# Delta-rule attention with two expert layers: filler kept up by a modelled share, group 2 prepared sooner, GpSimd steps told shorter to the planner, y keyed by group parity

## The chip, the cores and the metric

The kernel runs on one core of a Trainium2 chip. The time is device microseconds of one launch. Three runs of the kernel before took 1090.52, 1092.03 and 1093.01 us; the median is 1092.03 us.

## The reference

Three computations stand one behind the other. The first is a recurrence over 768 steps for 4 batches of 8 heads with a head dimension of 48:

```python
k_n = k / (norm(k, axis=-1, keepdims=True) + 1e-06)
for t in range(S):
    y[:, :, t] = einsum('bhd,bhde->bhe', q[:, :, t], state)
    v_old = einsum('bhde,bhd->bhe', state, k_n[:, :, t])
    state = state + beta[:, :, t] * outer(k_n[:, :, t], v[:, :, t] - v_old)
x = y.transpose(0, 2, 1, 3).reshape(3072, 384)
x = (silu(x @ w_gate) * (x @ w_val)) @ w_out        # d_ff 1536
out = elu(x @ w_in) @ w_out2                        # d_ff 2048
```

## The kernel before, in words

**Groups.** The 3072 tokens are taken in 12 groups of 256: 128 steps of two batches, in four parts of 32 steps; even and odd groups have different batches. For each group the attention turns the recurrence into triangular matrices of 32 by 32, one for each head, batch and part, which have to be inverted; then come the products with q, k and v, the state's update, and the transposed output, which is the input of the first expert layer. In the last eight groups the first expert layer takes two groups together. The second expert layer runs at the end, over tiles of 512 tokens.

**The steps of attention**, with the lines that the prediction speaks of. `norms` computes the lengths of the keys on VectorE: the sums at line 589, small Newton steps at 641 to 643, the scaling at 597. `prepare` transposes q and k on TensorE (line 698), forms the products of keys (line 748), masks them on VectorE (line 768), and has GpSimd scale and mask v and the matrices (lines 687, 805, 677, 812). `invert` transposes each matrix in four pieces on VectorE (line 852), then solves on GpSimd: 31 multiplications (line 869) and 31 additions (line 876), each waiting for the one before; this is the "chain" of a group. VectorE then transposes the result back (line 900). Group 0 is an exception: its inverse is made on VectorE in halves, which TensorE joins (lines 917 and 933, the "joining products"). `attention` multiplies with the inverse on TensorE (line 994, "xstep", 64 or 128 products of 32 rows), makes the output's and the state's factors ("gstep", line 1031, with VectorE's additions of q at line 1013), carries the state through the four parts of a group (line 1081, VectorE's update at line 1090), forms y (line 1121, "yall"), which ScalarE copies (line 1129), and transposes it (line 1164), after which it is split into a high and a low part (VectorE's at line 1179).

**Weights.** Weights of the first layer come as 18 tiles of 768 KB, loaded in halves on SP's queue (`load_w`, `half`), four halves in flight at most. Each tile is decoded to two fp32r tensors, a high and a low part: two passes on ScalarE, one on VectorE (line 1274), a copy on ScalarE (line 1284), a subtraction on VectorE (line 1288). From the first tile on, 12 "f-steps" of the expert layer follow for each group (`moe1`): products of the gate and the value half with the input's parts (line 1350, the first product with weights), SiLU on ScalarE (line 1358), the product of both halves on VectorE ("times", line 1361), a split of the result into high and low (ScalarE line 1369, VectorE line 1374), and nine output products (line 1382, "output product" of that step).

**The order.** Nothing of this runs in the order in which the code lists it. Each piece is a step with a priority (`add`), and `Order.run` puts the steps in order on each engine by a model: a step's cost on its engine, when its inputs and buffers come free, and the lowest priority number among those that can start. VectorE, ScalarE, GpSimd, TensorE and SP then each work in the order so found. The cost that is told for a step of the chain is

```python
[("POOL", SLOW[min(g, 3)] * (215 + 1.8 * n), SLOW[min(g, 3)] * (215 + 1.8 * n) + 80, 0, f)]
```

with n elements, `SLOW` being 1.0, 1.5, 1.4 and 1.1 for group 0, 1, 2 and all later ones. The preparation of a group has the priority `att_pri(g) - 5`, that of group 1 has `P1` = 14.7 and thereby stands ahead of the decoding of the weights, which has

```python
decode(n, tag, tk, att_pri(0) + 4.8 + 0.02 * n)
```

The loads of k, q and v of group 2 wait, in the order, for weight tile number `K2` = 5.

**Filler.** Where the model sees TensorE idle before a step, up to a modelled time `UNTIL`, `Order.run` puts products in whose result nobody uses: `fill` (line 1551, a 128x512 product), `quick` (line 1557) and `fill2`. Their number follows from the gap alone. The keys that the planner writes for y, `("yk", a)`, are the same for every group.

## Time and profile before

| | |
|---|---|
| median of three runs | 1092.03 us |
| the profiled execution | 1097.85 us, span 1096.1 us |
| instructions in it | 29901 |
| mean granted TensorE clock | 0.982 |
| DMA over the span | 57.07 MB, mean 52 GB/s |
| TensorE idle, by its own row | 1096.1 - 1077.4 = 18.7 us |

All rows below are of the one profiled execution; its time is 5.8 us over the median. PE is TensorE's matmul, DVE is VectorE, ACT ScalarE, POOL GpSimd, SP the engine that issues loads. "PEclk" is the clock that TensorE was granted as a share of full speed (2.4 GHz). In the timeline a row joins consecutive instructions of one line, and brackets tell the idle time ahead of it and what released it. Line numbers are those of the kernel before; in the changed kernel the same lines stand 23 to 27 lines further down.

### The profile page before, as it was taken

How to read it: one execution, taken by the hardware profiler on the slowest of the kernel's cores; microseconds unless marked ns; L12 is line 12 of the kernel's file. 1: busy time of each engine (PE TensorE's matmuls, PEld its weight loads, DVE VectorE, ACT ScalarE, POOL GpSimd, SP SyncE). 2: the span in 40 equal slices, each digit the busy share in tenths (PEclk: the TensorE clock that was granted, in tenths of full speed). 3: DMA queues.
4: the chain of work that ended last, by engine and by line, in shares of the span. 5: the costliest groups of instructions: out<-in, count | busy, mean ns of one | idle time of the engine just before them, and what ended most of it. 6: DMA issues, size and time to landing. Idle time of an engine off the chain costs nothing.

```text
span 1096.1 us, 29901 instructions
## 1 busy us (share of the span) xinstructions
PE 1077.4 (98%) x12839; PEld 937.1 (85%) x12839; DVE 602.8 (55%) x1178; ACT 537.6 (49%) x1076; POOL 342.2 (31%) x765
## 2 busy tenths in 40 slices
PE   8989999999999999999999999999999999999998
PEld 6678999999988787888777788888888888898887
DVE  7788766666555544556434466546345454444534
ACT  6679554344343433333322577645455454554443
POOL 1685777687770874064540000000000000000000
PEclk9589999999999999999999999999999999999999
DMA  9683131223012201203000456101001010000000
GB/s 164 162 245 103 31 47 31 33 45 58 5 27 35 45 2 38 38 16 60 9 19 2 154 191 198 44 1 48 11 1 58 1 58 1 10 29 1 29 1 29
DMA packets 104949, 57.07 MB, mean 52 GB/s; under 512 B 77392, under 2 KB 97360, under 8 KB 104816
## 3 DMA queue, kind: packets, MB, share of 16 engines
q1 hardware_dynamic: 104816, 55.16, 20.3%
q8 instruction: 100, 1.64, 0.6%
q14 instruction: 33, 0.27, 0.1%
HBM read 45.71 MB, written 9.44 MB: 50 GB/s over the span
## 4 chain that ended last, share of the span: by engine, by line
PE 90%; ACT 3%; DVE 3%; DMA 2%; issue 1%; SPq 0%; DVEq 0%; ACTq 0%
PE gv L1350 26%; PE acc L1382 11%; PE acc L1514 9%; PE gv L1476 9%; PE at L1476 9%; PE at L1514 9%; PE at L1081 3%; PE at L1031 3%; PE at L1382 3%; PE at L698 2%; PE at L994 2%; PE at L1121 1%; PE at L748 1%; DMA w<-in_moe_w_val_dram 1%; PE acc L1551 1%
## 5 line engine op out<-in xcount | busy, mean ns | idle before, releaser
L1350 PE MATMUL gv<-xa,w 128*128 128x512 f32 (+1 forms) x1008 | 218.6, 350 | 2.2 <-DVE hb L1374 1.1
L1350 PEld LDWEIGHTS gv<-xa,w 128*128 128x128 f32 x1008 | 160.3, 190 | 27.6 <-DVE hb L1374 3.2
L1382 PE MATMUL acc<-hb,w 128*128 128x256 f32 (+1 forms) x720 | 155.3, 335 | 0.0
L869 POOL TENSOR_TENSOR ain<-z,ain 128x126 f32<-128x126 f32 (+22 forms) x310 | 120.6, 389 | 67.6 <-DVE ain L852 32.5
L1350 PE MATMUL gv<-xb,w 128*128 128x256 f32 (+1 forms) x720 | 139.4, 327 | 0.0
L876 POOL TENSOR_TENSOR z<-z,ain 128x126 f32<-128x126 f32 (+22 forms) x310 | 128.0, 413 | 23.8
L1361 DVE TENSOR_TENSOR gv<-gv,tb 128x256 f32<-128x256 f32 (+1 forms) x96 | 54.1, 564 | 132.3 <-PE gv L1350 106.7
L1358 ACT ACTIVATE tb<-gv 128x256 f32<-128x256 f32 (+1 forms) x96 | 47.3, 492 | 157.6 <-PE gv L1350 157.4
L1350 PEld LDWEIGHTS gv<-xb,w 128*128 128x128 f32 x720 | 107.8, 190 | 12.6
L1382 PEld LDWEIGHTS acc<-hb,w 128*128 128x128 f32 x720 | 107.2, 191 | 12.7
L1369 ACT CAST hb<-gv 128x256 fp32r<-128x256 f32 (+1 forms) x96 | 46.0, 479 | 108.6 <-DVE gv L1361 105.7
L1374 DVE TENSOR_TENSOR hb<-gv,hb 128x256 fp32r<-128x256 f32 (+1 forms) x96 | 53.3, 555 | 42.4 <-PE at L1382 26.4
L1491 DVE SCALAR_TENSOR_TENSOR hb<-gv,hb 128x512 f32<-128x512 f32 x45 | 31.1, 691 | 81.2 <-ACT hb L1488 81.2
L1482 ACT ACTIVATE hb<-gv 128x512 f32<-128x512 f32 x45 | 26.9, 598 | 79.2 <-PE gv L1476 79.1
L1382 PE MATMUL at<-hb,w 128*128 128x512 f32 x144 | 56.2, 390 | 0.0
L1488 ACT ACTIVATE hb<-hb,zn 128x512 f32<-128x512 f32 x70 | 50.7, 724 | 2.2
L1491 DVE SCALAR_TENSOR_TENSOR hb<-at,hb 128x512 f32<-128x512 f32 x25 | 17.3, 692 | 60.6 <-ACT hb L1488 60.4
L1031 PEld LDWEIGHTS at<-gr,R 32*96 32x96 f32 x1292 | 39.0, 167 | 10.1 <-issue 5.9
L1482 ACT ACTIVATE hb<-at 128x512 f32<-128x512 f32 x25 | 15.0, 600 | 63.0 <-PE at L1476 62.9
L1031 PE MATMUL at<-gr,R 32*96 32x80 f32 x1292 | 44.8, 257 | 0.9 <-ACT lc L1050 0.9
L1485 ACT ACTIVATE hb<-hb 128x512 f32<-128x512 f32 x70 | 44.3, 633 | 2.1
L1476 PE MATMUL at<-lc,w 128*128 128x512 f32 x150 | 42.8, 393 | 0.0
(261 smaller groups left out, 2223.3 us busy)
## 6 DMA issues: line engine op xcount, KB each, us to landing
w<-in_moe_w_out_dram SPq DMA_DIRECT2D x28, 384.0 KB, 4.5
w<-in_moe_w_in_dram SPq DMA_DIRECT2D x16, 384.0 KB, 3.9
w<-in_moe_w_gate_dram SPq DMA_DIRECT2D x12, 384.0 KB, 4.2
w<-in_moe_w_val_dram SPq DMA_DIRECT2D x12, 384.0 KB, 4.7
kq<-in_q_dram SPq DMA_DIRECT2D x11, 384.0 KB, 6.1
x2d<-hb SPq DMA_DIRECT2D x16, 256.0 KB, 2.6
kp<-in_k_dram SPq DMA_DIRECT2D x10, 384.0 KB, 4.4
R<-in_v_dram SPq DMA_DIRECT2D x24, 96.0 KB, 2.2
```

Of the source, the lines that this page charges most:

```text
L869: E.tensor_tensor(out=t, in0=z[:, l:l + 1, x:y].to_broadcast([128, m, y - x]), in1=an[:, l + 1:32, l:l + 1].to_broadcast([128, m, y - x]), ...
L876: E.tensor_tensor(out=z[:, l + 1:32, x:y], in0=z[:, l + 1:32, x:y], in1=t, op=ALU.add)
L1031: PE.matmul(bank[h[c].got[0]][0:96, i:i + 80], lhsT=R[t, u, :], rhs=gr[t, u, o0:o0 + 80], start=True, stop=True, skip_group_check=True)
L1350: PE.matmul(dst, lhsT=wt[:, a_, kk * 128:(kk + 1) * 128], rhs=X[b_][:, :, kk, :] if two else X["one", g][:, b_, kk, :], start=(n == 0), st ...
L1358: A.activation(out=c['s'], in_=gate(0), func=ACTF.Silu)
L1361: V.tensor_tensor(out=gate(1), in0=gate(1), in1=c['s'], op=ALU.mult)
L1374: V.tensor_tensor(out=c['h'][1], in0=gate(1), in1=c['h'][0].bitcast(F32), op=ALU.subtract)
L1382: PE.matmul(sums(d), lhsT=wt[:, a_, d * 128:(d + 1) * 128], rhs=c['h'][b_], start=(f == 0 and n == 0 and (two or d != 1)), stop=(f == F1 - ...
L1476: PE.matmul(x, lhsT=W[f][:, 0, a_, kk * 128:(kk + 1) * 128], rhs=x2[n][b_][:, kk, :], start=(m == 0), stop=(m == 3 * KD - 1))
L1488: A.activation(out=c['r'], in_=c['r'], func=ACTF.Identity, bias=neg1, scale=1.0)
L1491: V.scalar_tensor_tensor(out=c['r'], in0=bank[h.got[0]], scalar=0.0, in1=c['r'], op0=ALU.max, op1=ALU.add)
L1514: PE.matmul(o, lhsT=c['h'][:, b_, t * 128:(t + 1) * 128], rhs=W[f][:, 1][:, a_, :], start=(f == 0 and m == 0), stop=(f == F2 - 1 and m == 2))
```

## The change

The planner keeps a list of what TensorE does in modelled time and weighs each kind of step by a factor (`FULL`). From 20 us of modelled time until the first product of the expert layer, it looks, ahead of each step of the attention, at the last 3413 ns of modelled time; where the weighed share is under `LOWEST` = 0.42 it adds as many fillers as lift it there, whether or not a gap is that long. `SLOW` becomes 1.25 and 1.1 for groups 1 and 2. The preparation of group 2 gets the priority 14.75, ahead of the decoding, and its loads wait for weight tile 6 instead of 5. The keys of y tell odd from even groups. In pairs of groups each product with the gate half is ordered behind the value half's product of the f-step before. `XTWO` is empty and so changes nothing.

```diff
--- before.py
+++ after.py
@@ -69,6 +69,10 @@
     BUSY = 4200.0
     SLOW = 1.8
     COLD = 430.0
+    LOWEST = 0.42
+    SPAN = 3413.0
+    KEEP = 20e3
+    FULL = (1.0, 1.0, 0.5, 0.15, 0.25, 0.2, 0.12, 0.06, 0.05)
 
     def __init__(self):
         self.rng = Random(self.SEED)
@@ -83,6 +87,8 @@
         self.cold = False
         self.last_end = 3e3
         self.since = 0.0
+        self.acts = []
+        self.dense = False
         self.steps = []
         self.last = {}
         self.seen = {}
@@ -165,6 +171,10 @@
     def link(self, b, o):
         b.succ.append(o)
         o.np += 1
+
+    def active(self, t):
+        return sum((min(b, t) - max(a, t - self.SPAN)) * w for a, b, w in self.acts[-60:]
+                   if b > t - self.SPAN and a < t)
 
     def run(self, until):
         self.until = until
@@ -246,6 +256,7 @@
                         self.fetch(t - gap, self.unit * n, 2 * n, True)
                         self.fill(n)
                         self.awake(t - gap, t - gap + self.unit * n)
+                        self.acts.append((t - gap, t - gap + self.unit * n, 1.0))
                         gap -= self.unit * n
                     n = int(self.BLOCK - self.at % self.BLOCK) // 4 * 2 + 4
                     self.fetch(t - gap, 28.0 * n, 2 * n, True)
@@ -254,9 +265,16 @@
                 unit = self.COLD if self.cold else self.unit
                 n = int((self.share if gap < 4000 else self.LONG) * gap / unit +
                         (0.5 if t < self.EARLY and not self.cold else 0.0))
+                keep = not self.dense and t > self.KEEP and o.pri[0] < 1000
+                if keep:
+                    short = self.LOWEST * self.SPAN - self.active(t) - max(0, n) * unit
+                    if short > 0:
+                        n = max(0, n) + int(short / unit + 0.7)
                 if n > 0:
-                    late = self.fetch(t - gap, gap, 2 * n, True)
+                    gap = max(gap, 0.0)
+                    late = self.fetch(t - gap, max(gap, n * unit), 2 * n, True)
                     self.awake(t - gap, t - gap + n * unit)
+                    self.acts.append((t - gap, t - gap + n * unit, 1.0))
                     t = max(t, t - gap + n * unit + late)
                     self.fill(n)
                     kind[0] = k[0]
@@ -281,6 +299,9 @@
                     end = t + lat
                     kind[0] = k[0]
             free[e] = t + occ
+            if e == "PE" and not self.dense:
+                self.acts.append((t, t + occ, self.FULL[k[0]]))
+                self.dense = o.pri[0] >= 1000
             for h in o.need:
                 a = sorted((slot.get(s, 0.0), i) for i, s in enumerate(h.pool)
                            if slot.get(s, 0.0) is not None)[:h.n]
@@ -317,7 +338,7 @@
     KD = DM // 128
     C = 4
     BLOCKED = (0,)
-    SLOW = (1.0, 1.5, 1.4, 1.1)
+    SLOW = (1.0, 1.25, 1.1, 1.1)
     PL1 = 0.5
     ND = 10
     UNTIL = 170e3
@@ -328,13 +349,15 @@
     CALM = 10
     WARM = 8
     P1 = 14.7
+    PREP = {1: P1, 2: 14.75}
     LATE = NW - 2
     LC0 = (NW - 3, NW - 1)
     PAIRS = 4
     THREE = 1
     XSHY = True
+    XTWO = ()
     XDVE = (0,)
-    K2 = 5
+    K2 = 6
     BIG = ()
 
     sb = ctx.enter_context(tc.tile_pool(name="sb", bufs=1))
@@ -979,7 +1002,7 @@
             return f
         o0, q0, k0_ = first_of(g), q_of(g), k_of(g)
         paired = g >= NB - 2 * PAIRS
-        for aa in [(0, 1)] if g and (not paired or XSHY) else [(0,), (1,)]:
+        for aa in [(0, 1)] if g and (not paired or XSHY and g not in XTWO) else [(0,), (1,)]:
             shy = paired and len(aa) == 2
             h = {(a, n): Slots(GB if shy else AT, 1) for a in aa for n in range(2)}
 
@@ -1142,8 +1165,8 @@
                 k0 = state(a, c)[1]
                 rk_ += [k0, (k0, 1)]
             def rest():
-                add(p, act(384, put), r=[h] + (yd if a else []), w=[yk[a], ("yk", a)], use=[h])
-            return 750, f, rk_ + lk[a] + INIT, h, [yk[a], ("yk", a)] + (yd if a else []), rest
+                add(p, act(384, put), r=[h] + (yd if a else []), w=[yk[a], ("yk", g % 2, a)], use=[h])
+            return 750, f, rk_ + lk[a] + INIT, h, [yk[a], ("yk", g % 2, a)] + (yd if a else []), rest
 
         def xtr(a):
             h = Slots(AT, 1)
@@ -1184,7 +1207,7 @@
             def rest():
                 add(p, act(384, hi), r=[h] + kh_, w=[("xh", g % 2, a)] + kh, use=[h])
                 add(p, dvp(384, lo), r=[h, ("xh", g % 2, a)] + kl_, w=[("xl", g % 2, a)] + kl, use=[h])
-            return (370, f, [("yk", a), yk[a]] + (yd if a else []), h,
+            return (370, f, [("yk", g % 2, a), yk[a]] + (yd if a else []), h,
                     kx + ([] if paired else [("xh", g % 2, a), ("xl", g % 2, a)]), rest, 6)
 
         def chains(c):
@@ -1315,6 +1338,7 @@
         if fresh:
             buf['sums'] = Slots(["at3"], 1)
         hs = buf.get('sums')
+        turned = []
 
         def sums(d):
             if two:
@@ -1384,7 +1408,8 @@
                                   skip_group_check=True)
             pp = p + f
             h1 = h[-1]
-            x = add(pp, pe(ns, proj(0), 1), r=xk + wk, w=[(h[0], 0)] + turn(4), need=h[:1] + ([hs] if fresh and f == 0 else []))
+            x = add(pp, pe(ns, proj(0), 1), r=xk + wk, w=[(h[0], 0)] + turn(4), need=h[:1] + ([hs] if fresh and f == 0 else []),
+                    after=turned[-1:])
             mark.setdefault((g, 'm'), x)
             add(P_MOE, act(w, silu), r=[(h[0], 0)], w=[ht] + turn(0), need=[ht], use=h[:1])
             if gs[-1] == NB - 1 and f == F1 - 1:
@@ -1392,6 +1417,8 @@
                     out=sm[2][:, 0:1], in_=neg1, func=ACTF.Exp))], r=["neg1", ht], w=["sm"])
             mark[gs[-1], 'last'] = add(pp, pe(ns, proj(1), 1), r=xk + wk, w=[(h1, 1)] + turn(5), need=h[1:],
                                        use=() if two else h[:1], after=[x])
+            if two:
+                turned.append(mark[gs[-1], 'last'])
             add(P_MOE, dvp(w, times), r=[ht], w=[(h1, 1)] + turn(1), use=[h1, ht])
             after = buf.get(('evac', g - 1), ()) if f == (0 if two else 2) else ()
             add(P_MOE, act(w, hi), r=[(h1, 1)], w=[(hh[0], 0)] + turn(2), need=hh[:1], use=[h1], after=after)
@@ -1586,7 +1613,7 @@
     rows()
     def ahead(g):
         load_k(g, 100 + 10 * g if g > 1 else PL1, [sent[K2]] if g == 2 else [])
-        norms(g, att_pri(g) - 5 if g > 1 else P1)
+        norms(g, PREP.get(g, att_pri(g) - 5))
 
     ahead(1)
     attention(0, att_pri(0) + 1)
@@ -1620,7 +1647,7 @@
         if g:
             if g > 1:
                 load_qv(g, 100 + 10 * g, [sent[K2]] if g == 2 else [])
-            prepare(g, att_pri(g) - 5 if g > 1 else P1)
+            prepare(g, PREP.get(g, att_pri(g) - 5))
             if g + 1 < NB:
                 ahead(g + 1)
             attention(g, att_pri(g) + 1 if g > 1 else P1)
```

What moves on the engines is told by the order of instructions. On VectorE, the place where group 2's inverse is transposed back (line 900; the names with z are the inverse, gv and hb the expert layer's intermediate results), in the kernel before:

```order
L768 TENSOR_TENSOR gr<-at_87,nbs 128x8x2x32
L768 TENSOR_TENSOR gr<-at_88,nbs 128x8x2x32
L1361 TENSOR_TENSOR gv_84<-gv_84,tb_2190 128x256
L1374 TENSOR_TENSOR hb_86_2205<-gv_84,hb_86_2205 128x256
L1361 TENSOR_TENSOR gv_83<-gv_83,tb_2218 128x256
L1374 TENSOR_TENSOR hb_88_2233<-gv_83,hb_88_2233 128x256
L900 STREAM_TRANSPOSE ain<-z_640 128x32x16
L852 STREAM_TRANSPOSE ain<-gr 128x256
```

The same place on VectorE in the changed kernel, where line 900 is now 923, 1274 is 1297, 1288 is 1311, 1361 is 1385 and 1374 is 1398:

```order
L1311 TENSOR_TENSOR w_70_1838<-xb_112,w_70_1838 128x2x384
L1398 TENSOR_TENSOR hb_73_1888<-gv_83,hb_73_1888 128x256
L1297 SCALAR_TENSOR_TENSOR xb_112<-xb_112,w_54_1512 128x768
L1113 TENSOR_TENSOR sv<-at_88,sv 48x2x4x48 x2
L1311 TENSOR_TENSOR w_74_1926<-xb_112,w_74_1926 128x2x384
L1297 SCALAR_TENSOR_TENSOR xb_112<-xb_112,w_57_1530 128x768
L1385 TENSOR_TENSOR gv_84<-gv_84,tb_1954 128x256
L923 STREAM_TRANSPOSE ain<-z_646 128x32x16
L1398 TENSOR_TENSOR hb_77_1984<-gv_84,hb_77_1984 128x256
L1311 TENSOR_TENSOR w_76_1971<-xb_112,w_76_1971 128x2x384
L1385 TENSOR_TENSOR gv_83<-gv_83,tb_1998 128x256
```

Before, the transposition stood behind the results of 14 f-steps, two of them of group 1's layer and all decoding done; now it stands behind 11, ahead of the split of the eleventh result (hb_77) and of the last weight tile's subtraction (w_76).

On TensorE, what stands in front of group 2's xstep (line 994) in the kernel before; acc<-hb is an output product, gv<-xb a first product with weights of group 1's layer:

```order
L1382 MATMUL acc<-hb_82_2081,w_75_1939 128x256 x9
L1350 MATMUL gv_84<-xb_2000,w_14_593 128x256 x18
L1350 MATMUL gv_83<-xb_2000,w_16_601 128x256 x18
L1382 MATMUL acc<-hb_86_2205,w_20_717 128x256 x9
L1350 MATMUL gv_84<-xb_2000,w_25_826 128x256 x18
L994 MATMUL at_86<-gr,ain 32x80 x4
```

In the changed kernel (1350 is 1374, 1382 is 1406, 994 is 1017, 1164 is 1187, 748 is 771), from the last output product of group 0's layer on:

```order
L1406 MATMUL acc<-hb_80_2017,w_76_1971 128x256 x9
L1187 MATMUL at_88<-ident,y_81_2109 128x128 x3
L1187 MATMUL at_86<-ident,y_82_2114 128x128 x3
L771 MATMUL at_87<-kq 32x64 x16
L771 MATMUL at_89<-kq 32x64 x16
L771 MATMUL at_87<-kq 32x64 x16
L771 MATMUL at_89<-kq 32x64 x16
L1374 MATMUL gv_84<-xb_2218,w_14_597 128x256 x18
L1017 MATMUL at_88<-gr,ain 32x80 x4
```

Two first products of 18 and one output product of nine of group 1's layer, which stood ahead of the xstep, now stand behind it: 45 products.

On TensorE at the opening, from the joining products (917, 933; now 940, 956) to the xstep of group 0 (now 1017), with the fillers (now 1578), in the changed kernel:

```order
L940 MATMUL at_86<-ain,gr 32x32 x32
L1578 MATMUL acc<-tb_64 128x512 x3
L956 MATMUL at_87<-z_509,ain 32x32 x32
L1578 MATMUL acc<-tb_64 128x512 x3
L956 MATMUL at_88<-z_509,ain 32x32 x32
L1578 MATMUL acc<-tb_64 128x512 x2
L1017 MATMUL at_89<-gr,ain 32x80 x4
```

The kernel before had two fillers there, between the two pieces of line 933. From there to the first product with weights there are 42 in 17 places where there were 21 in nine; the nine fillers right ahead of the first joining product are the same.

## Rows read from the trace of the kernel before

**Rows 1.** The page, busy time of each engine over the span.

```profile
PE 1077.4 (98%) x12839; PEld 937.1 (85%) x12839; DVE 602.8 (55%) x1178; ACT 537.6 (49%) x1076; POOL 342.2 (31%) x765
```

**Rows 2.** Windows: stretch, its length, busy of each engine, PEclk, DMA, GB/s.

```profile
25.60:56.30 30.70, 29.32 (x615) 21.65 (x606) 23.51 (x50) 19.01 (x40) 18.66 (x33) 0.50 0.65 160
63.17:66.58 3.41, 3.41 (x17) 2.96 (x16) 3.30 (x9) 2.74 (x5) 3.02 (x6) 0.50 0.61 185
135.87:1096.10 960.23, 953.80 (x10490) 829.02 (x10489) 496.62 (x936) 442.73 (x887) 261.93 (x612) 1.00 0.16 39
```

**Rows 3.** Timeline of PE: start us, us, engine line op out<-in xcount [idle before].

```profile
21.05 2.33 PE L1551 MATMUL acc<-tb 128*128 128x512 f32 x9
...
36.49 1.22 PE L1551 MATMUL acc<-tb 128*128 128x512 f32 x2
...
40.04 2.08 PE L1551 MATMUL acc<-tb 128*128 128x512 f32 x4
...
62.83 0.62 PE L1164 MATMUL at<-ident,y 128*128 128x128 f32 x3 [2.85 <-ACT y L1129]
...
66.68 3.46 PE L1350 MATMUL gv<-xa,w 128*128 128x256 f32 x27
```

**Rows 4.** Windows of GpSimd's chains of groups 1, 2 and 3.

```profile
34.34:75.79 41.45, 37.06 (x594) 29.61 (x593) 31.38 (x66) 29.11 (x56) 35.12 (x65) 0.66 0.75 212
...
93.66:131.40 37.74, 36.39 (x716) 34.12 (x715) 29.72 (x61) 26.25 (x62) 33.11 (x65) 1.00 0.34 85
139.50:170.20 30.70, 30.59 (x659) 28.92 (x662) 19.88 (x49) 14.72 (x41) 26.07 (x65) 1.00 0.28 42
```

**Rows 5.** The same windows, VectorE's line 1274 alone, then 1288 (third alike).

```profile
34.34:75.79 41.45, 7.09 (x7) 0.66 0.75 212
...
93.66:131.40 37.74, 3.80 (x4) 1.00 0.34 85
139.50:170.20 30.70, 0.00 (x0) 1.00 0.28 42
...
34.34:75.79 41.45, 7.71 (x9) 0.66 0.75 212
...
93.66:131.40 37.74, 6.09 (x6) 1.00 0.34 85
```

**Rows 6.** Timeline of GpSimd, in and behind group 1's chain.

```profile
47.37 0.83 POOL L687 TENSOR_TENSOR gr<-l,nbs 128x384 f32<-128x384 f32 x1 [1.71 <-PE at L1031]
...
75.75 2.17 POOL L805 TENSOR_TENSOR gr<-gr,strict 128x256 f32<-128x256 f32 x2
...
79.47 1.30 POOL L812 TENSOR_TENSOR gr<-gr,strict 128x512 f32<-128x512 f32 x1
93.66 0.26 POOL L869 TENSOR_TENSOR ain<-z,ain 128x31 f32<-128x31 f32 x1 [12.89 <-DVE ain L852]
```

**Rows 7.** Groups by line on VectorE, 93.6 to 131.4 us: busy, mean ns | idle.

```profile
L1361 DVE TENSOR_TENSOR gv<-gv,tb 128x256 f32<-128x256 f32 x7 | 3.0, 423 | 2.9 <-ACT tb L1358 2.9
...
L1090 DVE TENSOR_TENSOR st<-at,sv 48x384 f32<-48x384 f32 x2 | 1.1, 555 | 0.0
L1179 DVE TENSOR_TENSOR xb<-at,xb 128x384 fp32r<-128x384 f32 x2 | 1.1, 554 | 0.0
L589 DVE TENSOR_REDUCE sm<-kq 128x8 f32<-128x384 f32 x2 | 1.0, 536 | 0.0
```

**Rows 8.** Timeline of VectorE.

```profile
121.97 0.32 DVE L641 SCALAR_TENSOR_TENSOR sm<-sm,sm 128x16 f32<-128x16 f32 x1
...
125.43 0.33 DVE L597 TENSOR_TENSOR nbs<-sm,nbt 128x16 f32<-128x16 f32 x1
...
134.43 1.16 DVE L900 STREAM_TRANSPOSE ain<-z 128x512 f32<-128x512 f32 x1
```

**Rows 9.** Timeline of PE at group 2's xstep.

```profile
133.62 2.32 PE L1350 MATMUL gv<-xb,w 128*128 128x256 f32 x18
135.87 1.63 PE L994 MATMUL at<-gr,ain 32*32 32x80 f32 x128
```

## The prediction

> **What bounds the kernel now.** I read the page first. TensorE (PE) is busy in 1077.4 of 1096.1 us [rows 1], so time can only come from a slower clock, from filler, or from the 18.7 us of idle. The stretches place it: from 135.87 us to the end PE is idle for 960.23 - 953.80 = 6.4 us in all [rows 2], and before that one stretch stands out, 25.6 to 56.3 us, at a granted clock of 0.50 (1.2 of 2.4 GHz) with PE busy in 29.32 of 30.70 us [rows 2]. What can be won lies ahead of 135.87 us, where PE starts the fourth-stage product of group 2 ("xstep", line 994). So I measure the change at that point: when does it start, and how much work has PE done by then?
>
> The timeline shows what the slow clock did. From 36.49 us (filler behind the first "gstep") on PE works without a break until the clock rises at 56.3, and fillers stand between the attention's small products; four of them take 2.08 us at 40.04, while nine took 2.33 us at the full clock at 21.05 [rows 3]. The first product with weights starts at 66.68 us [rows 3].
>
> The second resource is GpSimd, which inverts one group after another in 62 dependent steps. The same chain (with two further steps in it) takes 41.45, 37.74 and 30.70 us for groups 1, 2 and 3 [rows 4]. VectorE's decoding of weights (lines 1274 and 1288) runs beside it 7 + 9 = 16 times in the first, 4 + 6 = 10 times in the second, not at all in the third [rows 5]. Taking out 1.71 us of waiting in group 1 [rows 6], the excess over 30.70 is 9.04 and 7.04 us, or 16.08 / 26 = 0.62 us for each decoding instruction. Between the two chains GpSimd has 17.9 us, of which 12.89 are a wait for VectorE's transpositions [rows 6].
>
> **The change, part by part.**
>
> *Fillers.* Between the first joining product and the first product with weights there are 42 where there were 21 (counted in the order). In the stretch from the first gstep to the first "yall" it is 16 in both. Its part from 36.49 to 56.3 took 19.8 us, all at half clock; at full clock the same list takes 10. So if the clock holds, the first product with weights comes at 66.7 - 10 = 56.7 us. The additional fillers ahead of gstep lie where PE waits for ScalarE's copies of the group's inverse anyway; I cost them at nothing, and at 9 x 0.25 = 2.3 us if that cover is gone. If the clock doesn't hold the gain is 0 to 2 us. I take it that it holds.
>
> *Group 2 ahead of the decoding, GpSimd told shorter.* These move VectorE's instructions. Its transposition of group 1's inverse (line 900) now stands after four f-steps of the first expert layer instead of five, that of group 2 after 11 instead of 14, and the latter now stands ahead of the split of f-step 10's result and of the last decoding. VectorE works in order, so both wait for GpSimd, and PE's output product of step 10, with all behind it, waits for them. I therefore add up GpSimd:
>
> - Group 1 starts when its fourth transposition is done, as before at 34.34 us [rows 4]: the order ahead of it is the same, but for one short copy that now stands behind.
> - 14 decodings lie ahead of its line 900 in the new order once it has started: 30.70 + 14 x 0.62 = 39.4, so it ends at 73.7. (The 1.71 us wait is gone, since gstep is over earlier.)
> - The five steps behind it (masks and scaling of v) took from 75.79 to 80.77 = 5.0 us [rows 6]: 78.7. Group 2's transpositions are in by then: the last stands four short instructions behind line 900.
> - Group 2 starts at 78.7, at once; 19 decodings lie between the two lines 900: 30.70 + 19 x 0.62 = 42.5. It ends at 121.2 us (131.4 before [rows 4]).
>
> Is anything else later? PE: 56.7, then 90 + 27 weight products at 0.125 (18 in 2.25 us, 133.62 to 135.87 [rows 9]) = 14.6, and 3.4 of attention: 74.7; it then needs line 900 of group 1 and the split, 73.7 + 1.2 + 0.4 = 75.3. From there 27 products, 3.4, bring xstep of group 1 to 78.7. Up to output product 10 come 29.2 us more: 162 weight products 20.3, xstep 1.6 [rows 9], the rest some 7.3 (estimate); so PE is there at 107.9. VectorE has 34 us of work between the two lines 900 (19 decodings of 1.0 [rows 5], 14 short ones of 0.42 [rows 7], some 9 of attention): 73.7 + 1.2 + 34 = 108.9. Both are there 12 us before GpSimd.
>
> Behind 121.2 the new order demands, on VectorE, before PE may take group 1's first weight product: 1.16 (line 900 [rows 8]), 3 x 0.42 (lines 1374 and 1361 [rows 7]), 1.0 (1288 [rows 5]), 1.1 (589, twice [rows 7]), 3.8 (the small steps from 641 to 597: 121.97 to 125.76, with their gaps [rows 8]), 0.4 for the two ahead of them (estimate), 1.1 (1090) and 1.1 (1179) [rows 7] = 11.0; then 18 products, 2.2. Xstep of group 2 starts at 121.2 + 13.2 = 134.4. At that point 36 + 9 = 45 products are undone that were done before, 5.6 us. So the comparison is 140.0 against 135.87 [rows 9]: **+4.1 us**. In the new order everything is even if GpSimd ends group 2 at 117.1.
>
> The rule of GpSimd's shared interfaces can be set beside this. The rows count only decoding: 16, 10 and 0 instructions for 9.04, 7.04 and 0 us. The Trainium skill, GPSIMD Engine Reference, Key points, says that GpSimd contends with VectorE's instructions that run in a two-port mode or have two inputs in SBUF; by that the four additions of q (line 1013) in each chain count too, 34 instead of 26, 0.47 us each, and with 18 and 23 such group 2 ends at 120.1, an estimate 1.1 us earlier, and the sum is +3.0 instead of +4.1. That rule speaks against telling GpSimd's steps shorter while decoding is packed closer.
>
> *PE's wait and its clock.* PE stands from about 109 to 122.8 us. In the trace 3.4 us at 0.50 follow upon a wait of 2.85 us (for y, at 62.83) [rows 2, 3]. Dense work at half clock loses half its time, at most 1.7 us per such stretch; most is hidden behind VectorE's 11 us. I take +0.5; bounds 0 and 3.4.
>
> *The rest.* K2 = 6 moves the load of k (one issue, 384 KB) and q behind one weight half each. The weight half that was behind them issues sooner; no term, since no weight is last in a step above. The own keys of y and the chained pair products change the order from group 4 on, where PE's idle time is 6.4 us to the end: no gain above 1 us; a loss is bounded by one new stall, 2.9 us as the longest of before. I take 0. Group 3's chain (30.7 us, from about 136) ends at 167, PE's next 36 us of work (before: xstep of group 2 to that of group 3) at 170: no wait.
>
> Sum: +4.1 + 0.5 = +4.6 us on the profiled execution (1097.85 us, span 1096.1). The median of runs is 1092.03, 5.8 us below that; the same step on it gives **1096.6 us**, own range 1092 to 1099 (0.62 per decoding may be 0.5 to 0.7: 33 of them make -4 to +2.6).
>
> **The rivals.**
>
> *Faster: GpSimd isn't last.* If packed decodings cost GpSimd half of 0.62 us (20 of its us become 10), line 900 of group 2 runs when VectorE comes to it, 108.9. Then xstep starts at 122.1, with 5.6 undone 127.7: -8.2, and with a little given back in decoding -8, **1084 us**. For it: GpSimd's spans are rough in a profile, and the 0.62 rests on two chains. Against: 9.04 / 16 = 0.57 and 7.04 / 10 = 0.70 lie close together, and the third chain, without decoding, is the shortest. It decides at an end of group 2's chain below 115.
>
> *Slower still: the clock does not hold.* For it: from 25.6 to 56.3 it stayed at 0.50 with PE busy in 96% of the time, fillers included [rows 2], so being busy alone did not lift it, and the fall at 25.6 came behind nine fillers [rows 3] that the change leaves alone. Against: nine of the 21 additional fillers stand ahead of the first gstep, right behind the place where it fell. Then the first weight product comes at about 65, line 900 of group 1 at 81.5, group 2's chain starts at 85 instead of 78.7 and ends near 127.5: +10, **1102 us**. It decides when group 2's chain starts later than 80.
>
> *No difference.* Order changes that end level: group 2's chain ends between 115 and 119.5: 1090 to 1094.
>
> **How the numbers follow.** Forecast 0.50, faster 0.25, clock not held 0.13, no difference 0.12. A measurement of this kernel tells 0.2% (2.2 us) from no change. Faster by more: 0.25; within: 0.20 (all of the last case, a part of the forecast's lower end); slower: 0.55. The range reaches from the faster case's time to the slower one's, 1084 to 1102.
>
> **What would show it.** Right: granted clock near 1.0 from 25 to 56 us; first weight product at 55 to 58; GpSimd's chains without a break between, group 2's ending near 121; VectorE's line 900 of group 2 and PE's output product 10 waiting for GpSimd, PE idle for some 10 us between 105 and 130. Wrong: that line 900 without a wait, PE filled through 100 to 130 us, or a chain of group 2 shorter than 37 us with 19 decodings beside it.

## The result, and the profile after

The changed kernel is slower: 1104.78 us median of four runs (1102.55 to 1106.81), 1.0118 times the kernel before (interval 1.0104 to 1.0132), +13.2 us where +4.6 was forecast and 1102 was the end of the range. The direction was right, and so was the mechanism (VectorE and then TensorE wait for GpSimd's chain of group 2); the size was not.

First what came as forecast. The page of the changed kernel, busy time of each engine, answers to [rows 1]:

```profile
span 1103.2 us, 30005 instructions
...
PE 1073.2 (97%) x12890; PEld 934.5 (85%) x12890; DVE 606.0 (55%) x1181; ACT 535.7 (49%) x1073; POOL 349.5 (32%) x765
```

TensorE's idle time has risen from 18.7 to 1103.2 - 1073.2 = 30.0 us, although its products with weights begin earlier. The windows of the changed kernel (columns as in [rows 2]) place it:

```profile
25.60:56.30 30.70, 27.12 (x721) 19.88 (x720) 28.20 (x60) 23.78 (x48) 21.40 (x35) 1.00 0.71 188
80.00:95.00 15.00, 11.81 (x146) 10.62 (x147) 11.77 (x17) 13.18 (x29) 13.43 (x21) 0.89 0.45 140
110.00:125.00 15.00, 5.36 (x41) 5.16 (x40) 6.20 (x11) 3.79 (x9) 11.62 (x28) 0.80 0.12 20
125.00:140.00 15.00, 15.00 (x475) 13.93 (x475) 9.71 (x30) 6.21 (x17) 1.67 (x3) 0.85 0.09 29
140.00:1103.20 963.20, 955.84 (x10393) 832.60 (x10391) 495.72 (x933) 440.76 (x882) 261.39 (x609) 1.00 0.16 39
```

The clock held from 25.6 to 56.3 us, as taken. TensorE then stood for 9.6 of the 15 us from 110 on, and for 3.2 us from 80 to 95. Its timeline in the changed kernel (line 1374 is the first product with weights, 1406 the output product, 1017 the xstep):

```profile
113.75 0.52 PE L1406 MATMUL acc<-hb,w 128*128 128x256 f32 x3
...
123.91 1.65 PE L1406 MATMUL acc<-hb,w 128*128 128x256 f32 x6 [9.64 <-DVE w L1311]
...
133.95 2.42 PE L1374 MATMUL gv<-xb,w 128*128 128x256 f32 x18
136.29 1.89 PE L1017 MATMUL at<-gr,ain 32*32 32x80 f32 x128
```

The first product with weights came at 55.76 us (56.7 forecast); the wait at output product 10 ended at 123.91 (122.8 forecast). VectorE's timeline, at group 1 (73.99) and at group 2 (from 121.50), shows whom it waited for:

```profile
73.99 1.19 DVE L923 STREAM_TRANSPOSE w<-w 128x512 f32<-128x512 f32 x1 [1.79 <-POOL w L899]
...
121.50 1.09 DVE L923 STREAM_TRANSPOSE ain<-z 128x512 f32<-128x512 f32 x1 [8.77 <-POOL z L899]
122.46 0.39 DVE L1398 TENSOR_TENSOR hb<-gv,hb 128x256 fp32r<-128x256 f32 x1
122.77 1.08 DVE L1311 TENSOR_TENSOR w<-xb,w 128x768 fp32r<-128x768 f32 x1
...
129.67 1.12 DVE L1113 TENSOR_TENSOR st<-at,sv 48x384 f32<-48x384 f32 x2 [2.06 <-PE at L1104]
```

Line 923 (900 before) waits 8.77 us for GpSimd's last step, and the split of f-step 10 and the last weight's subtraction wait behind it in VectorE's order. GpSimd's chains ended where the price of a decoding had put them. The chains in the changed kernel, groups 1, 2 and 3, answering to [rows 4]:

```profile
33.16:73.96 40.80, 38.39 (x731) 32.58 (x732) 34.92 (x73) 31.69 (x59) 36.17 (x65) 1.00 0.79 223
78.15:121.46 43.31, 32.74 (x528) 30.33 (x527) 31.09 (x45) 32.49 (x68) 38.69 (x66) 0.93 0.30 75
139.54:170.20 30.66, 30.15 (x648) 28.41 (x653) 20.14 (x50) 14.13 (x40) 26.04 (x65) 1.00 0.28 42
```

With 14 and 19 decodings beside them they ended at 73.96 and 121.46; 73.7 and 121.2 were forecast.

### The profile page after: what moved, and what is told of

Its sections match the earlier page's. It is cut to its first block, busy times and chain, and to the rows that moved or that the text cites. A ratio compares the mean times of both kernels' runs of the same rounds, so it can differ in the third digit from the quotient of the medians.

```text
span 1103.2 us, 30005 instructions
## 1 busy us (share of the span) xinstructions
PE 1073.2 (97%) x12890; PEld 934.5 (85%) x12890; DVE 606.0 (55%) x1181; ACT 535.7 (49%) x1073; POOL 349.5 (32%) x765
## 4 chain that ended last, share of the span: by engine, by line
PE 91%; POOL 4%; ACT 2%; issue 1%; DVE 1%; DMA 0%; DVEq 0%; POOLq 0%; ACTq 0%
PE gv L1374 26%; PE acc L1406 11%; PE acc L1541 9%; PE gv L1503 9%; PE at L1503 9%; PE at L1541 9%; PE at L1104 3%; PE at L1054 3%; PE at L1406 3%; PE acc L1578 2%; PE at L721 2%; PE at L1144 2%; PE at L771 2%; PE at L1017 1%; POOL w L899 1%
## 5 line engine op out<-in xcount | busy, mean ns | idle before, releaser
L899 POOL TENSOR_TENSOR z<-z,ain 128x126 f32<-128x126 f32 (+22 forms) x310 | 134.3, 433 | 23.9
L1406 PEld LDWEIGHTS acc<-hb,w 128*128 128x128 f32 x720 | 108.0, 192 | 24.4 <-DVE w L1311 10.4
L1054 PEld LDWEIGHTS at<-gr,R 32*96 32x96 f32 x1352 | 36.5, 159 | 10.3 <-issue 4.2
L1054 PE MATMUL at<-gr,R 32*96 32x80 f32 x1352 | 42.3, 249 | 1.6 <-POOL z L899 1.6
```

The costliest lines, as they stand in the source:

```text
L899: E.tensor_tensor(out=z[:, l + 1:32, x:y], in0=z[:, l + 1:32, x:y], in1=t, op=ALU.add)
L1054: PE.matmul(bank[h[c].got[0]][0:96, i:i + 80], lhsT=R[t, u, :], rhs=gr[t, u, o0:o0 + 80], start=True, stop=True, skip_group_check=True)
L1406: PE.matmul(sums(d), lhsT=wt[:, a_, d * 128:(d + 1) * 128], rhs=c['h'][b_], start=(f == 0 and n == 0 and (two or d != 1)), stop=(f == F1 - ...
```

## What was wrong: the point that it was compared with

The rows ahead of the prediction are of one execution of 1097.85 us. The first experiment is that kernel again, unchanged.

**before_again.** No edit.

> The kernel before, unchanged, to see where its time stands against its profiled execution (1097.85 us, clock 0.982, TensorE at half clock from 25.6 to 56.3 us) and its median (1092). Theory: that long stretch at half clock is not in every execution; in those near 1091 us it is shorter and the granted clock of the run is above 0.982 (0.988 to 0.995). Rival: every execution has that stretch, the clock is 0.982 in each, and the first profile was 6 us slow for another reason.

Measured: 1.0007 (0.9986 to 1.0028); ten runs from 1089.98 us at a granted clock of 0.991 to 1097.85 us at 0.982. The execution on which the prediction rests, 1097.85 us too, was as slow as the slowest of these ten. The one profiled now took 1091.49 us. Its windows:

```profile
25.60:56.30 30.70, 23.85 (x752) 17.64 (x740) 27.63 (x57) 23.56 (x49) 20.29 (x30) 0.83 0.65 165
80.00:95.00 15.00, 13.63 (x300) 12.93 (x298) 13.64 (x21) 12.95 (x27) 9.86 (x15) 1.00 0.47 141
110.00:125.00 15.00, 15.00 (x316) 14.54 (x304) 10.58 (x28) 6.65 (x16) 12.65 (x31) 1.00 0.13 30
125.00:140.00 15.00, 15.00 (x314) 14.32 (x313) 9.51 (x22) 7.23 (x25) 9.89 (x25) 1.00 0.09 21
140.00:1089.80 949.80, 943.74 (x10222) 819.85 (x10220) 489.53 (x920) 436.90 (x868) 254.30 (x596) 1.00 0.16 40
```

and of its TensorE the first product with weights and group 2's xstep:

```profile
61.83 3.38 PE L1350 MATMUL gv<-xa,w 128*128 128x256 f32 x22
...
130.21 1.64 PE L994 MATMUL at<-gr,ain 32*32 32x80 f32 x128
```

From 25.6 to 56.3 us the mean clock is 0.83, not 0.50 [rows 2]: with the same instructions the stretch at half clock is shorter. The first product with weights comes at 61.83 instead of 66.68 [rows 3], the xstep at 130.21 instead of 135.87 [rows 9]. So the clock that the change holds was worth 61.83 - 55.76 = 6 us, not 11, and the comparison that decides reads: 136.29 + 5.6 for 45 undone products - 130.21 = +11.7 of the 13.4 us between the two profiled executions (1104.90 and 1091.49). The last 1.7 us lie behind: TensorE idles for 963.20 - 955.84 = 7.4 us from 140 us to the end, against 949.80 - 943.74 = 6.1, and what is left is small differences along 950 us.

A third execution bears this out. The kernel of tail_only (below) has the opening of the kernel before and took 1092.28 us; its window, its first product with weights and its xstep:

```profile
25.60:56.30 30.70, 25.79 (x747) 19.16 (x740) 26.54 (x55) 22.75 (x48) 19.24 (x30) 0.71 0.62 157
...
62.53 4.16 PE L1351 MATMUL gv<-xa,w 128*128 128x256 f32 x27
...
130.94 1.63 PE L994 MATMUL at<-gr,ain 32*32 32x80 f32 x128
```

And the xstep is the right place to compare at. If 0.125 us, the prediction's price, is added to its start for each product with weights that the kernel before has done by then and this one has not (and taken off for each done in addition), the time of every profiled execution lies 961 to 965 us behind it, those of filler_back and told_16_late_far apart, whose traces are not drawn on.

## The experiments on the parts

**fill_add.** The fillers alone, on the order of the kernel before; the planner's own times are left as they were:

```diff
+                extra = 0
+                if not self.dense and t > self.KEEP and o.pri[0] < 1000:
+                    short = self.LOWEST * self.SPAN - self.active(t) - max(0, n) * unit
+                    if short > 0:
+                        extra = int(short / unit + 0.7)
...
+                if extra:
+                    self.fill(extra)
```

> The order of the kernel before, with the change's rule for fillers alone: 13 more of them in the opening, nothing else moved (the planner's clock is not told of them). Theory: the granted clock is near 1.0 from 25 to 56 us and the first product with weights comes at 57 to 59 us; against executions of before that hold the clock anyway the time is the same, 1089 to 1093, against those that do not it is up to 5 us shorter. Rival: fillers are the cost of the change, and this is 3 us or more slower than before.

Measured: 0.9996 (0.9977 to 1.0016). In its profile the first product with weights comes at 60.08 us and the mean clock from 25.6 to 56.3 is 0.89, so the stretch at half clock is shortened and not gone. Neither a gain nor a cost can be told: the fillers aren't the loss, and a gain from the clock that they hold, if there is one, lies within the 0.2% of this measurement.

**fill_gap.** The order of the changed kernel, with only those fillers that the gap calls for:

```diff
+                told = n
                 if keep:
...
-                    self.fill(n)
+                    self.fill(max(0, told))
```

> The order of the changed kernel without its 16 additional fillers (those of the gap rule stay). Theory: the clock falls to a half behind the joining products, the first product with weights comes at 60 to 66 us instead of 55.8, the inverse of group 2 ends 4 to 9 us later than 121.4, and the time is 1108 to 1113 us. Rival: the fillers are part of the loss; then it is faster than 1104.8 by 2 us or more.

Measured: 1108.44 us, 1.0139 (1.0114 to 1.0165), 3.7 us over the changed kernel. Its clock from 25.6 to 56.3 is 0.75, the first product with weights comes at 57.82 and line 923's wait for group 2 ends at 123.64, 2.1 us later than with the fillers. The direction and the time are those of the theory; both places moved less than it said (60 to 66 us, and 4 to 9 us later). In this order the fillers help.

**tail_only.** The own keys of y and the ordered pair products on the kernel before:

```diff
-        add(p, act(384, put), r=[h] + (yd if a else []), w=[yk[a], ("yk", a)], use=[h])
+        add(p, act(384, put), r=[h] + (yd if a else []), w=[yk[a], ("yk", g % 2, a)], use=[h])
...
+                    after=turned[-1:])
```

> The kernel before with the own keys of y and the ordered pair products alone: the opening is as before, only the order from group 4 on moves. Theory: no change, 1090 to 1093.5, since TensorE is idle for 6.4 us in all behind 136 us. Rival: the tail of the change costs 2 us or more, a part of the 13 us.

Measured: 1.0000 (0.9980 to 1.0020). These two parts, costed at nothing, cost nothing that shows (within 0.2%). `K2` = 6, costed at nothing too, is not in this kernel.

**slow_only.** GpSimd told shorter (with the keys of y and the ordered pair products), the rest as before:

```diff
-    SLOW = (1.0, 1.5, 1.4, 1.1)
+    SLOW = (1.0, 1.25, 1.1, 1.1)
```

> The shorter costs told for GpSimd (and the keys of y) alone: no added fillers, group 2 prepared as before, K2 at 5. 468 products with weights stand ahead of group 2's xstep, line 923 of group 2 behind 17 f-steps. Theory: no wait for GpSimd at group 2, at most 2 us at group 1's inverse, which now stands behind 3 f-steps instead of 5; 1090 to 1096. Rival: a wait of 5 us or more at group 1's inverse, and above 1097.

Measured: 1094.09 us, 1.0018 (0.9997 to 1.0039). Line 923 waits 2.17 us at group 1 and not at all at group 2, where 468 products stand ahead of the xstep. Here, with that much work ahead of the chain's end, the short price did no harm that shows.

**filler_back.** All of the change but the added fillers:

```diff
-    LOWEST = 0.42
+    LOWEST = 0.0
```

> The change with the added share of fillers turned off for the planner too (LOWEST = 0), all the rest of it kept. The order then has 441 products with weights ahead of group 2's xstep where the changed kernel has 342, and VectorE's line 923 of group 2 stands behind 16 f-steps instead of 11. Theory: the shorter costs told for GpSimd and the earlier preparation cost nothing by themselves, because here line 923 comes to VectorE after the chain has ended; no wait over 2 us for GpSimd at it, and 1090 to 1095. Rival: the two are the loss whatever the fillers do; then it stays above 1099.

Measured: 1098.15 us, 1.0043 (1.0021 to 1.0064), over the theory's end and under the rival's. It differs from slow_only in the earlier preparation of group 2 and in `K2` = 6 alone, so the 4.1 us between the two (1098.15 and 1094.09) come with these. Its trace is of an execution of 3594.0 us, so none tells where they are lost, nor which of the two parts loses them; that stays open.

## The experiments on the wait

**late.** One step held back: the transposition of group 2's inverse is put down only when TensorE's xstep needs it, with the steps that must follow it.

```diff
+            if o in later and e == "PE":
+                for y in queue:
+                    y()
+                queue, later = [], set()
+            if o is self.late or o in later:
+                queue.append(f)
+                later.update(o.succ)
+            else:
+                f()
...
```

> The changed kernel with one instruction moved on VectorE: the transposition back of group 2's inverse (line 923) stands right ahead of the product that needs it, behind the rest of group 0's work (with group 3's clearing of the result's buffer, which has to follow it). TensorE's order is untouched. Theory: TensorE's wait of 9.6 us at the output product of step 10 goes, what is behind it runs while GpSimd finishes, xstep of group 2 starts at 126 to 129 us instead of 136.3, and the time is 1095 to 1098 us. Rival: the wait only moves to the xstep or to another of VectorE's results; then it stays above 1102 us.

Measured: 1099.27 us, 1.0055 (1.0035 to 1.0075): 5.5 us back, not the 7 to 10 of the theory. The wait of 9.64 us is gone, but another of 2.77 us stands ahead of group 1's first product, whose 18 products then take 4.21 us and not 2.42, and the xstep comes at 130.43:

```profile
126.29 4.21 PE L1386 MATMUL gv<-xb,w 128*128 128x256 f32 x18 [2.77 <-ACT xb L1209]
130.43 2.21 PE L1029 MATMUL at<-gr,ain 32*32 32x80 f32 x128
```

ScalarE's timeline in late tells why:

```profile
124.30 0.20 ACT L693 COPY far<-sm 128x8 f32<-128x8 f32 x1 [3.43 <-POOL R L710]
...
125.15 0.49 ACT L1209 CAST xb<-at 128x384 fp32r<-128x384 f32 x1
```

A copy of 0.2 us for group 3 (line 693) writes a buffer that GpSimd reads for group 2 right behind its chain (line 710). It waits 3.43 us for that, and the split of group 1's input (line 1209) behind it. The chain still set the pace, by a second way.

**late_far.** Those three copies are held back too:

```diff
+            if g == 3:
+                od.late += (x,)
...
```

> As late, and ScalarE's three small copies of group 3's factors (into the buffer that GpSimd reads for group 2 behind its chain) also stand behind, right ahead of group 2's xstep, so that ScalarE's split of group 1's input no longer waits behind them for GpSimd. Theory: in late GpSimd still sets the pace through those copies; TensorE's wait of 2.77 us before group 1's first product and the half clock behind it go, xstep of group 2 starts at 124 to 127 us instead of 130.4, and the time is 1093.5 to 1097. Rival: the copies only took the blame; xstep stays at 130 and the time at 1099.

Measured: 1094.43 us, 1.0015 (0.9999 to 1.0031). TensorE's timeline in late_far:

```profile
121.68 1.71 PE L783 MATMUL at<-kq 48*32 48x64 f32 x128
123.32 2.42 PE L1388 MATMUL gv<-xb,w 128*128 128x256 f32 x18
125.77 1.79 PE L1031 MATMUL at<-gr,ain 32*32 32x80 f32 x128
```

The xstep comes at 125.77, 10.5 us earlier than in the changed kernel, and the time falls by 10.4 of 13.2 us. TensorE's own order is the same in all three kernels: 10.4 us of the loss were one transposition and three small copies that stood too early on VectorE and ScalarE.

**told_16.** The same without holding anything back, by telling the planner a longer time for group 2's chain, about what it took:

```diff
-    SLOW = (1.0, 1.25, 1.1, 1.1)
+    SLOW = (1.0, 1.25, 1.6, 1.1)
```

> The changed kernel with group 2's steps told with 1.6 instead of 1.1, nothing held back. Line 923 of group 2 then stands behind 12 f-steps and all decoding instead of 11 f-steps and 17 of 18 tiles. Theory: one f-step more (2.3 us of products) is not enough against a wait of 8.8 us on VectorE; TensorE still stands for 5 to 8 us, and the time is 1099 to 1104. Rival: what stands behind line 923 decides and not how far it is, so that with the last decoding ahead of it the wait goes as in late; 1094 to 1098.

Measured: 1095.26 us, 1.0017 (0.9994 to 1.0041). The rival's time, though not quite by its words: the count of f-steps (12 instead of 11) said nothing of the place, since the planner had put the whole attention of group 1 and the masks of group 3 ahead of line 923 as well. VectorE's timeline in told_16:

```profile
120.63 0.56 DVE L1202 TENSOR_TENSOR xb<-at,xb 128x384 fp32r<-128x384 f32 x1
121.75 0.56 DVE L1202 TENSOR_TENSOR xb<-at,xb 128x384 fp32r<-128x384 f32 x1 [0.56 <-ACT xb L1197]
122.56 1.29 DVE L791 TENSOR_TENSOR gr<-at,nbs 128x512 f32<-128x512 f32 x2 [0.26 <-PE at L771]
123.77 1.15 DVE L923 STREAM_TRANSPOSE ain<-z 128x512 f32<-128x512 f32 x1
```

Line 923 waits for nobody, and the xstep stands at 126.20:

```profile
126.20 1.64 PE L1017 MATMUL at<-gr,ain 32*32 32x80 f32 x128
```

So one number, 1.1 for group 2 where 1.6 takes the wait away, carries 9.5 of the 13.2 us; but only together with the rest of the change, since with the same 1.1 slow_only loses nothing that shows.

**told_17.** As told_16 with 1.7, whose order has 396 products ahead of the xstep.

> As told_16, with 1.7 for group 2: told that late an end of the chain, the planner puts 396 products with weights ahead of group 2's xstep (351 with 1.6, 387 in the kernel before), line 923 behind the masks of group 3. Theory: told_16 already waits for nothing at line 923, so 45 products more ahead of the xstep fill what TensorE had left open there, and the time is 1089 to 1094, at or under the kernel before. Rival: with the weights decoded by 112 us nothing is left open in told_16, xstep comes 5 us later for the same work, and the time is that of told_16, 1094 to 1097.

Measured: 1096.36 us, 1.0037 (1.0018 to 1.0056): the rival. The xstep comes at 133.28, 7.1 us later than in told_16 for 45 more products:

```profile
133.28 1.63 PE L1017 MATMUL at<-gr,ain 32*32 32x80 f32 x128
```

No version that keeps the whole computation beats the kernel before. A version with both told_16's number and the held-back steps (told_16_late_far) does not keep all of the computation, and its 1104.48 us, for which 1091.5 to 1096 were expected, are not drawn on.

**no_dec.** VectorE's two instructions for each weight cut to 8 columns:

```diff
-            V.scalar_tensor_tensor(out=c['t'], in0=c['t'], scalar=3, in1=pr()[:, :, :, 0],
+            V.scalar_tensor_tensor(out=c['t'][:, :, 0:4], in0=c['t'][:, :, 0:4], scalar=3, in1=pr()[:, :, 0:4, 0],
...
-            return lambda: e.tensor_tensor(out=W[n][:, :, 1, :], in0=c['f'],
+            return lambda: e.tensor_tensor(out=c['w'][:, :, 1, 0:4], in0=c['f'][:, :, 0:4],
```

> The changed kernel in its own order, with VectorE's two instructions of each weight's decoding cut to 8 of 768 columns, and both parts of each product read from the high part (so low bits and low parts of the weights are left out). Theory: these instructions stretch GpSimd's steps; the chains of groups 1 and 2 take 30.5 to 33 us each instead of 40.8 and 43.3, group 2's inverse ends before 106 us, line 923 waits for nothing, xstep of group 2 starts before 125 us and the time is 1087 to 1093. Rival: GpSimd is slowed by something else (transfers, ScalarE, the clock); then the chains stay above 38 us.

Measured: 1087.55 us in one run. GpSimd's chains of groups 1, 2 and 3 in no_dec:

```profile
31.92:63.65 31.73, 30.26 (x557) 24.87 (x558) 20.45 (x66) 26.97 (x53) 26.04 (x65) 1.00 0.78 206
73.19:105.61 32.42, 30.08 (x511) 28.09 (x511) 15.72 (x45) 30.33 (x64) 25.14 (x65) 0.95 0.41 109
122.20:153.14 30.94, 30.60 (x677) 28.81 (x675) 19.77 (x51) 14.46 (x40) 26.32 (x65) 1.00 0.27 41
```

40.80 and 43.31 us became 31.73 and 32.42, with transfers as dense as in the changed kernel (DMA shares 0.78 and 0.41 against 0.79 and 0.30) and ScalarE's decoding left in. So the decoding on VectorE is what stretches the chains. Line 923 does not wait for GpSimd at group 2, and the xstep comes at 119.15:

```profile
119.15 1.63 PE L1017 MATMUL at<-gr,ain 32*32 32x80 f32 x128
```

That time is under every run of the kernel before, but it is one run with less work on VectorE; the kernel before was not run with the same cut, so it isn't shown that the changed order would then be the faster one.

## Why the prediction was right and wrong, by its steps

- *Fillers hold the clock.* Right for the profiled execution of the changed kernel (1.00 from 25.6 to 56.3 us, 55.76 us for the first product), though not for all: with the same fillers it was 0.88 there in late's. Over the profiles read here the added fillers do lift it: 0.88 to 1.00 in seven executions with them, 0.50 to 0.83 in five without. Wrong in what the gain was set against: "its part from 36.49 to 56.3 took 19.8 us, all at half clock" is true of that execution and not of the one profiled again. The step that failed is the last one, "the same step on it" (on the median): nearly all of the 5.8 us by which the execution stood over the median was that stretch at half clock, and the change could not win it a second time. The gain of the fillers was mis-sized by 135.87 - 130.21 = 5.7 us.
- *GpSimd's chains.* Right within 0.3 us at both ends, partly by two errors that cancel. The excess over 30.66 is (40.80 - 30.66) / 14 = 0.72 and (43.31 - 30.66) / 19 = 0.67 us for each decoding, above the 0.62 taken; and each chain began earlier than taken (33.16 and 78.15 instead of 34.34 and 78.7), so that the hit on the end is in part luck.
- *What waits behind.* Right: the split of step 10, the last decoding, the output product, 9.64 us of idle time. VectorE and TensorE came there at 112.7 and 114.3 us, not 108.9 and 107.9, which cost nothing since GpSimd was later still. Behind 121.46 the path took 14.8 us to the xstep and not 13.2. The mean clock was 0.80 and 0.85 in the two stretches that hold it, and VectorE, behind which the slow clock was to be hidden, itself waited 2.06 us for TensorE's products of line 1104. So the xstep came 1.9 us later than forecast, of which 0.5 us were in the sum.
- *The 45 undone products.* Held as a term of the comparison: 136.29 + 5.6 - 130.21 gives 11.7 of the 13.4 us.
- *The rest at nothing.* The keys and the pair products cost nothing that shows by themselves (tail_only); `K2` was not run alone (with the earlier preparation it is the 4.1 us between filler_back and slow_only). 1.7 us between the two profiles lie behind the xstep.
- Sum of the misses: 5.7 + (1.9 - 0.5) + 1.7 = 8.8, which is 13.4 - 4.6.
- *The rivals.* "GpSimd isn't last" is out by its own sign, an end of group 2's chain below 115 us (121.46), and by no_dec. "The clock does not hold" did not happen (group 2's chain began at 78.15, before 80), though with the clock down (fill_gap) the time is 3.7 us longer still. "No difference" is what the change becomes with 1.6 told.

The Trainium skill, GPSIMD Engine Reference, Key points, was set against the count of decodings in the prediction: by its rule the additions of q count as well. The trace agrees with the rule, as the rows of the last section show. But chains 1, 2 and 3 have four such additions each, in the kernel before as in the changed one, so they are in the third chain's time already, and counting them beside it put the estimate at 120.1 instead of 121.2, where 121.46 was measured.

## What to carry to other kernels

Before a saving is added to a median, see whether the profiled execution has lost that very time by chance: a run that is 0.5% above the median, with half clock in a stretch that the change is to mend, counts the gain twice. Where a planner orders an engine that works in order, a price that is told too short can cost much: the step that waits stands ahead of work that could have run, and holds all of it. Here 1.1 instead of 1.6 cost 9.5 us, and 1.7 instead of 1.6 cost 1.1 us, which the intervals do not tell from nothing; what as large an error on the long side would cost was not tried. When such a wait is moved, look on the other engines for small instructions that wait for the same chain, since that second way may hold half of the loss (4.8 of 10.4 us here).

## What was not expected of the hardware

How GpSimd's steps are stretched can be seen instruction by instruction. GpSimd's timeline in the changed kernel, from 91 us on:

```profile
92.03 1.97 POOL L899 TENSOR_TENSOR z<-z,ain 128x110 f32<-128x110 f32 x1
94.07 0.44 POOL L892 TENSOR_TENSOR ain<-z,ain 128x126 f32<-128x126 f32 x1
...
95.10 0.42 POOL L892 TENSOR_TENSOR ain<-z,ain 128x120 f32<-128x120 f32 x1
95.60 0.43 POOL L899 TENSOR_TENSOR z<-z,ain 128x120 f32<-128x120 f32 x1
...
97.49 2.10 POOL L892 TENSOR_TENSOR ain<-z,ain 128x126 f32<-128x126 f32 x1
```

and VectorE's in the same stretch:

```profile
91.91 0.94 DVE L1297 SCALAR_TENSOR_TENSOR xb<-xb,w 128x768 int32<-128x768 int32 x1
92.78 0.94 DVE L1311 TENSOR_TENSOR w<-xb,w 128x768 fp32r<-128x768 f32 x1
...
95.01 0.89 DVE L1075 COPY dt<-at 96x320 f32<-96x320 f32 x2
...
97.03 0.41 DVE L1398 TENSOR_TENSOR hb<-gv,hb 128x256 fp32r<-128x256 f32 x1
97.36 0.67 DVE L1036 TENSOR_TENSOR dt<-dt,kq 48x512 f32<-48x512 f32 x1
97.96 0.48 DVE L1075 COPY l<-at 96x320 f32<-96x320 f32 x1
98.36 0.94 DVE L1311 TENSOR_TENSOR w<-xb,w 128x768 fp32r<-128x768 f32 x1
```

The same step of 126 columns takes 0.44 us or 2.10 us. It is not slowed in proportion: in both places the long step (110 columns in the first, 126 in the second) ends 0.3 us after an instruction of VectorE does (92.03 + 1.97 = 94.00 behind 92.78 + 0.94 = 93.72; 97.49 + 2.10 = 99.59 behind 99.30). The Trainium skill, SBUF — State Buffer, SBUF: two separate sides, says that an instruction of VectorE with two inputs in SBUF and one of GpSimd exclude each other for the whole instruction, whichever starts first; the rows of both places agree, and in the second the addition of q (line 1036) is among the instructions that hold GpSimd up. What was not expected is that one step of GpSimd is held through two of VectorE's instructions: in the second place 0.33 us lie between the end of line 1036 (98.03) and line 1311 (98.36), and the step did not get through there. The copy of line 1075 that VectorE runs in between does not explain it by itself: beside two such copies, from 95.01 us on, GpSimd's steps took 0.42 and 0.43 us. Why the step did not start in that gap stays open.

The second is the spread of the clock. With the same instructions the kernel before was granted between 0.982 and 0.991 of the full clock over ten executions, and took 1097.85 and 1089.98 us at the ends; how long the clock stays at its low level in the opening is not settled by the program (means of 0.50, 0.83 and, in tail_only with the same opening, 0.71 from 25.6 to 56.3 us). Added fillers do not end the spread: told_16 took 1093.02 to 1099.79 us.
